# Gates, keys and queries of steps 10 to 23 turned by VectorE in 32x32 squares instead of by TensorE

## The chip, the core and the metric

The kernel runs on one core of a Trainium2 chip. The core's engines work side by side, each through its own queue of instructions in order: TensorE (PE, with its weight loads as PEld) multiplies matrices into the eight banks of PSUM, VectorE (DVE), ScalarE (ACT) and GpSimd (POOL) work on elements, SyncE (SP) issues the transfers from and to memory. [...] The metric is the device time of one execution in microseconds (us).

## The reference

Three stages follow each other, for 4 batches of 768 tokens (3072 in all), 8 heads of 48 features, model width 384:

```python
# attention with a gated state, per batch and head
f = 1 / (1 + exp(-f_logit))
for t in range(768):
    state = f[t, :, None] * state + outer(k[t], v[t])
    y[t] = q[t] @ state
x = y as (3072 tokens, 384)
# first network: 384 -> 2048 -> 384
h = x @ w_in;  x = (h * cos(h)) @ w_out
# second network: rms norm, 384 -> 1536 -> 384
xn = x / sqrt(mean(x * x) + 1e-6) * rms_g
g = xn @ w_gate
out = (g * sigmoid(g) * (xn @ w_val)) @ w_out2
```

## The kernel before

**Steps.** The attention runs in 24 steps of 128 tokens (6 to a batch), all 8 heads at once as four pairs, with the features of a pair on the 128 partitions (48 of each 64 used) and the tokens along the row. Gates, keys and queries lie in memory token by token, so each has to be turned. For that they are loaded as tiles `nat` with the tokens on the partitions, unused columns holding 16.0 (`load_nat`), two transfers to a tensor, and TensorE turns them with four 128x128 transposes each into a bank of PSUM (`turn1`, L198). From there a step does: `guard_f` (L214, ScalarE: sums up what is below the least gate allowed; at the end the sum decides between this program and a general one), `gates` (tanh, L219), `scan_end` (VectorE: the affine step from tanh to sigmoid L228, a scan from the last token backwards into `E` L229, two tiny instructions; GpSimd copies the scan's end, L234), `scan_start` (a scan of the gates, L238; GpSimd copies parts of v, L239), `scale_k` and `scale_q` (keys and queries times the scans, L246 and L253), the products on TensorE (`piece_pe`), the masked copy of the scores (`causal`, L390), the new state and its decayed copy, and the step's result split in two parts, `xh` and `xl`.

**Blocks and slots.** The first network works on blocks of 512 tokens (four steps), each in 16 slots, one for 128 hidden units. Steps 0 to 4 of the attention run ahead; steps 5 to 23 are spread over the slots of blocks 0 to 4, one of four pieces of a step to a slot. A slot's actions are written out in the string `SLOT[1]` (for blocks 1 to 4), and each engine gets its instructions in the order of that string:

- H: nine matmuls for the hidden units (L550), in one of two banks in turn; k, w, s, g: the rounding of the cosine's argument on ScalarE (L559), the rest on VectorE (L565), the cosine on ScalarE (L571), the product with H's bank on VectorE (L576), which then is free for the H two slots on
- hi and lo, a slot later: g in two parts, gh on ScalarE (L584) and gl on GpSimd (L591)
- P: the attention's piece on TensorE
- out: nine matmuls for the output, of the hidden units two slots back (L601), from gh and gl. They end a slot and aren't in the string
- kn, xh, xl, am, st, kt, qt, cy, tanh, grd, scan: what the attention does on the other engines after the piece of the slot before
- act, dv, pe, po: work put off to a slot of a given number, such as the evacuation of a finished block (`m1_evac`, L613, ScalarE, in slot 2 of the block after), its squares, and the column sum on TensorE (`m1_sum`, L628)

With n0 and p0 the step and piece of the slot before, the four slots of a step are called A to D here. **A** (p0 = 0): P is the scores (L301); kn; tanh, guard and `scan_end` of step n0+1. **B** (p0 = 1): P is the new state (L326; none in a batch's last step) and the turn of the next keys; the masked copies, `scan_start`. **C** (p0 = 2): P is the result (L344 to L362) and the turn of the next queries; `scale_k`, the state's addition. **D** (p0 = 3): P is the turn of the scaled keys (L291; none in a batch's last step) and the turn of the next gates; xh, xl, `scale_q`, the state's decay.

The attention's products and turns share three banks in rotation (`att_bank`; the column sum takes one, too). SP's queue holds all transfers in the order in which the program issues them: with each turn the load of the same tensor two steps on, the load of v, and the small transfers for the norm.

Of the kernel before, what the change touches and what calls it, by code (L numbers as in the profile page):

```python
# [9 lines left out]
F32 = mybir.dt.float32  # L10
# [3 lines left out]
AF = mybir.ActivationFunctionType  # L14
ALU = mybir.AluOpType
# [13 lines left out]

SLOT = (  # L30
    "tanh hi H t kn x kt xh xl qt cy am st scan P k f w x grd f s t lo g po",
    "tanh hi H kn kt xh xl qt cy am st scan P k w grd s lo act dv g pe po",
    "act H hi k w lo P dv t pe s x g f po",
)
SLOT2 = (
# [14 lines left out]
def kernel(  # L50
# [14 lines left out]
    nc = tc.nc  # L65
    B, H, S, D = q.shape
# [3 lines left out]
    C = 128  # L70
    NP = H // 2
    NCH = S // C
    NSTEP = B * NCH
# [3 lines left out]
    GT = 4  # L77
# [44 lines left out]
    att = ExitStack()  # L122
    ap_ = att.enter_context(tc.tile_pool(name="ap", bufs=1))
    HEAD = 4
    nats = [ap_.tile([128, KD, 512], F32, name=f"nat{x}") for x in range(2)]
    ft = [ap_.tile([128, NP * W + 1], F32, name="ft")]
    c1 = ap_.tile([128, NP * W + 1], F32, name="c1")
# [10 lines left out]
    def body(t):  # L138
        return t[:, 0:NP * W].rearrange("p (i t) -> p i t", i=NP)[:, :, 1:W]
# [39 lines left out]
    def load_nat(n, parts=range(3)):  # L179
# [4 lines left out]
        for x in parts:  # L184
            src = (f_logit, k, q)[x]
            for j in range(2):
                a = src[b, j::2, t0:t0 + C, :].rearrange("i t d -> t i d")
                nc.sync.dma_start(out=nat(n)[:, x, :, j, 0:D], in_=a)

    def turned(n, x):  # L190
        return bank[x] if n <= HEAD else st[n, "t", x]

    def turn1(n, x):

        if n > HEAD:
            st[n, "t", x] = att_bank()
        for i in range(NP):
            nc.tensor.transpose(  # L198
                turned(n, x)[:, C * i:C * (i + 1)],
                nat(n)[:, x, i].rearrange("p j e -> p (j e)"), ident,  # L200
            )

    def turn(n):
        for x in range(3):
# [4 lines left out]
    def heads(t):  # L209
        return t.rearrange("p (i t) -> p i t", i=NP)  # L210

    def guard_f(n):
        x = heads(turned(n, 0))
        nc.scalar.activation(  # L214
            out=x, in_=x, func=AF.Relu, scale=-1.0, bias=cb[:, 3:4], accum_out=low[:, n:n + 1]
        )

    def gates(n):
        nc.scalar.activation(  # L219
            out=body(ft[0]), in_=heads(turned(n, 0)), func=AF.Tanh, scale=0.5  # L220
        )

    def scan_end(n):

        f = ft[0]
        E = ap_.tile([128, NP * W], F32, tag="E", name="E")
        st[n, "E"] = E
        nc.vector.tensor_scalar(body(f), body(f), 0.5, 0.5, op0=ALU.mult, op1=ALU.add)  # L228
        nc.vector.tensor_tensor_scan(  # L229
            E[:, ::-1], f[:, NP * W:0:-1], c1[:, NP * W:0:-1], 0.0, op0=ALU.mult, op1=ALU.add  # L230
        )
        nc.vector.tensor_scalar(pads(d1), pads(E), P_LEAST, None, op0=ALU.max)
        nc.vector.reciprocal(out=pads(d1), in_=pads(d1))
        nc.gpsimd.tensor_copy(out=pall[:, n, :], in_=pads(E))  # L234

# [7 lines left out]

    def scale_k(n):
        kt = ap_.tile([128, NP, C], F32, tag="kt", name="kt", bufs=2)
        nc.vector.tensor_tensor(  # L246
            out=kt, in0=heads(turned(n, 1)), in1=body(st.pop((n, "E"))), op=ALU.mult
        )
        st[n, "kt"] = kt

    def scale_q(n):
        qt = ap_.tile([128, NP, C], F32, tag="qt", name="qt", bufs=2)
        nc.vector.tensor_tensor(  # L253
            out=qt, in0=heads(turned(n, 2)), in1=body(ft[0]), op=ALU.mult
        )
        nc.vector.memset(pads(ft[0]), 0.0)
        st[n, "qt"] = qt

# [27 lines left out]
    def piece_pe(n, p):  # L286
        if p == 0:
            if not last(n):
                t = st[n, "tr"] = att_bank()
                for i in range(NP):  # L290
                    nc.tensor.transpose(t[:, 128 * i:128 * (i + 1)], st[n, "kt"][:, i, :], ident)  # L291
            if n >= HEAD and n + 1 < NSTEP:
                turn1(n + 1, 0)
                load_nat(n + 3, (0,))
                load_v(n + 1)
        elif p == 1:
            t = [att_bank(), att_bank()]
            for i in range(NP):
                for j in range(2):
                    o = 64 * j  # L300
                    nc.tensor.matmul(  # L301
                        t[j][:, C * i:C * (i + 1)], st[n, "kt"][o:o + D, i, :],
                        st[n, "qt"][o:o + D, i, :], start=True, stop=True,
                    )
            st.pop((n, "kt"))
            st[n, "sc"] = t
        elif p == 2:
            zs(n)
            if n >= HEAD and n + 1 < NSTEP:
                turn1(n + 1, 1)  # L310
                load_nat(n + 3, (1,))
        else:
            ys(n)
            if n >= HEAD and n + 1 < NSTEP:
                turn1(n + 1, 2)
                load_nat(n + 3, (2,))

    def zs(n):
        if last(n):
# [461 lines left out]
    if True:  # L781
# [120 lines left out]
        for j, (t0, N) in enumerate(blocks):  # L902
# [21 lines left out]
            for i in range(N1):  # L924
# [7 lines left out]
                    "hi": lambda: gp and m1_hi(*gp),  # L932
                    "lo": lambda: gp and m1_lo(*gp),
                    "kn": lambda: p0 == 0 and not last(n0) and kn_evac(n0),
                    "tanh": lambda: p0 == 0 and more and gates(n0 + 1),
                    "grd": lambda: p0 == 0 and more and guard_f(n0 + 1),
                    "scan": lambda: more and (
                        p0 == 0 and scan_end(n0 + 1) or p0 == 1 and scan_start(n0 + 1)
                    ),
# [313 lines left out]
```

## Time and profile before

| | |
|---|---|
| median of 3 runs | 1054.02 us (1053.69 to 1055.05) |
| the profiled execution | 1053.78 us |
| its span, first to last instruction | 1052.0 us |
| TensorE busy | 1012.3 us (96%) |
| VectorE busy | 576.1 us (55%) |
| ScalarE busy | 421.3 us (40%) |
| GpSimd busy | 321.0 us (31%) |
| chain that ended last | TensorE 86%, VectorE 5%, ScalarE 2%, transfers 2% |

The busy time of TensorE is an average over stages, and since matmuls overlap, the length of a single one isn't what it adds to the queue. That is read from the distance between the starts of two neighbours.

### The profile page before, as it was taken

Reading aid. Unit: us, or ns where it says so; the run is one execution under the profiler, and the core shown is the slowest. Engines: PE = TensorE matmul, PEld = TensorE weight load, DVE = VectorE, ACT = ScalarE, POOL = GpSimd, SP = SyncE. Lnnn points to the kernel's source line nnn. Section 1 sums busy time; section 2 is a strip of 40 time slices with the busy share of each in tenths; the row PEclk is TensorE's granted clock in tenths of the full one; section 3 lists DMA queues with packets and bytes.
Section 4 is the critical chain, followed back from the end, with each engine's and each line's share of the span. In section 5 each row is a group of like instructions: output and inputs, shape, how many; then the busy total and the mean of one; then the engine's idle time right before and its main releaser. Section 6 shows DMA issues by size and latency. Waiting matters only on the chain.

```text
span 1052.0 us, 15791 instructions
## 1 busy us (share of the span) xinstructions
PE 1012.3 (96%) x6088; PEld 829.4 (79%) x6088; DVE 576.1 (55%) x904; ACT 421.3 (40%) x737; POOL 321.0 (31%) x366
## 2 busy tenths in 40 slices
PE   6778899999999999999999999999999999999997
PEld 5556677777777777777787788888888888888886
DVE  7888875555556655554377766435335335335222
ACT  2466655444444444444477554322222212212211
POOL 1555654432533433253377453201001001001000
PEclk9798999999999999999999999999999999999999
DMA  8865222121212212110234344332342343342000
GB/s 173 192 177 134 87 51 61 31 39 36 63 32 44 61 31 38 38 47 3 48 118 132 104 150 150 86 118 88 124 142 82 114 130 94 120 127 60 31 1 34
DMA packets 144016, 89.24 MB, mean 85 GB/s; under 512 B 110902, under 2 KB 123190, under 8 KB 143932
## 3 DMA queue, kind: packets, MB, share of 16 engines
q1 hardware_dynamic: 143932, 88.14, 31.7%
q8 instruction: 50, 0.82, 0.3%
q14 instruction: 34, 0.28, 0.1%
HBM read 78.66 MB, written 9.46 MB: 84 GB/s over the span
## 4 chain that ended last, share of the span: by engine, by line
PE 86%; DVE 5%; ACT 2%; DMA 2%; issue 2%; POOL 1%; SPq 1%; DVEq 0%; ACTq 0%; POOLq 0%
PE bank L703 29%; PE bank L601 17%; PE bank L550 16%; PE bank L739 14%; PE bank L198 2%; PE bank L301 1%; PE bank L350 1%; PE bank L344 1%; DMA nat<-in_k_dram 1%; DVE E L229 1%; PE bank L362 1%; PE bank L326 1%; PE bank L291 1%; POOL gl L591 1%; DMA v_sb<-in_v_dram 1%
## 5 line engine op out<-in xcount | busy, mean ns | idle before, releaser
L601 PE MATMUL bank<-gh,wo 128*128 128x512 f32 x576 | 206.8, 413 | 1.5 <-ACT x L613 1.2
L591 POOL TENSOR_TENSOR gl<-g,gh 128x512 fp32r<-128x512 f32 x96 | 126.7, 1320 | 167.0 <-ACT gh L584 163.8
L717 DVE SCALAR_TENSOR_TENSOR u<-bank,sg 128x512 f32<-128x512 f32 x72 | 49.7, 691 | 199.2 <-PE bank L703 199.2
L601 PEld LDWEIGHTS bank<-gh,wo 128*128 128x128 f32 x576 | 109.3, 190 | 28.1 <-ACT x L613 2.5
L703 PE MATMUL bank<-xh,wo 128*128 128x512 f32 x360 | 122.8, 395 | 0.0
L601 PE MATMUL bank<-gl,wo 128*128 128x512 f32 x288 | 115.8, 402 | 4.7 <-POOL gl L591 4.6
L712 ACT ACTIVATE sg<-bank 128x512 f32<-128x512 f32 x72 | 43.1, 599 | 171.8 <-PE bank L703 171.8
L687 POOL TENSOR_TENSOR xl<-x2b,xh 128x512 fp32r<-128x512 f32 x18 | 24.2, 1344 | 283.1 <-ACT xh L686 283.1
L724 ACT CAST uh<-u 128x512 fp32r<-128x512 f32 x72 | 44.7, 621 | 152.4 <-DVE u L717 152.2
L576 DVE SCALAR_TENSOR_TENSOR g<-bank,wrap 128x512 f32<-128x512 f32 x96 | 66.3, 691 | 69.4 <-ACT wrap L571 67.7
L565 DVE SCALAR_TENSOR_TENSOR wrap<-bank,kint 128x512 f32<-128x512 f32 x96 | 65.8, 685 | 69.8 <-ACT kint L559 69.7
L559 ACT ACTIVATE kint<-bank,cb 128x512 int32<-128x512 f32 x96 | 65.9, 687 | 83.4 <-PE bank L550 83.2
L571 ACT ACTIVATE wrap<-wrap,cb 128x512 f32<-128x512 f32 x96 | 69.5, 724 | 72.8 <-DVE wrap L565 70.9
L584 ACT CAST gh<-g 128x512 fp32r<-128x512 f32 x96 | 59.6, 621 | 92.2 <-PE bank L601 70.3
L703 PEld LDWEIGHTS bank<-xh,wo 128*128 128x128 f32 x360 | 67.6, 188 | 14.6
L730 DVE TENSOR_TENSOR ul<-u,uh 128x512 fp32r<-128x512 f32 x72 | 51.6, 716 | 48.9 <-ACT uh L724 48.9
L739 PE MATMUL bank<-wo,uh 128*128 128x384 f32 x288 | 74.1, 338 | 0.0
L703 PE MATMUL bank<-xl,wo 128*128 128x512 f32 x180 | 71.0, 394 | 0.0
L601 PEld LDWEIGHTS bank<-gl,wo 128*128 128x128 f32 x288 | 54.7, 190 | 18.8 <-POOL gl L591 7.8
L198 PE MATMUL bank<-ident,nat 128*128 128x128 f32 x288 | 45.8, 284 | 13.7 <-DVE xl L382 4.0
L739 PEld LDWEIGHTS bank<-wo,uh 128*128 128x128 f32 x288 | 52.6, 188 | 3.5 <-issue 0.5
L525 POOL TENSOR_TENSOR wo<-wx,wo 128x384 fp32r<-128x384 f32 x32 | 35.9, 1122 | 52.4 <-ACT wo L524 52.4
(334 smaller groups left out, 2190.8 us busy)
## 6 DMA issues: line engine op xcount, KB each, us to landing
stage<-in_moe_w_out_dram SPq DMA_DIRECT2D x56, 384.0 KB, 3.3
stage<-in_moe_w_gate_dram SPq DMA_DIRECT2D x24, 384.0 KB, 3.2
stage<-in_moe_w_val_dram SPq DMA_DIRECT2D x24, 384.0 KB, 3.7
stage<-in_moe_w_in_dram SPq DMA_DIRECT2D x16, 384.0 KB, 3.6
nat<-in_f_logit_dram SPq DMA_DIRECT2D x48, 96.0 KB, 3.8
nat<-in_k_dram SPq DMA_DIRECT2D x48, 96.0 KB, 2.8
nat<-in_q_dram SPq DMA_DIRECT2D x48, 96.0 KB, 2.2
v_sb<-in_v_dram SPq DMA_DIRECT2D x24, 192.0 KB, 3.7
```

Of the source, the lines that this page charges most:

```text
L198: nc.tensor.transpose(turned(n, x)[:, C * i:C * (i + 1)], nat(n)[:, x, i].rearrange("p j e -> p (j e)"), ident,)
L550: nc.tensor.matmul(t, l[:, 128 * kk:128 * (kk + 1)], r[:, kk, 0:N], start=idx == 0, stop=idx == 3 * KD - 1,)
L559: nc.scalar.activation(out=kt, in_=hb[j, i], func=AF.Identity, scale=INV2PI * UNIT, bias=cb[:, 0:1])
L565: nc.vector.scalar_tensor_tensor(out=w, in0=hb[j, i], scalar=INV2PI * UNIT, in1=kt, op0=ALU.mult, op1=ALU.subtract)
L571: nc.scalar.activation(out=w, in_=w, func=AF.Sin, scale=2.0 * math.pi, bias=cb[:, 1:2])
L576: nc.vector.scalar_tensor_tensor(out=g, in0=hb.pop((j, i)), scalar=UNIT, in1=w, op0=ALU.mult, op1=ALU.mult)
L584: nc.scalar.copy(out=h, in_=g)
L591: nc.gpsimd.tensor_tensor(out=l, in0=g, in1=h.bitcast(F32), op=ALU.subtract)
L601: nc.tensor.matmul(acc[m][:, 0:N], lw[:, cs], r, start=i == 0 and x == 0, stop=i == N1 - 1 and x == 2,)
L703: nc.tensor.matmul(t[y], l[:, 128 * kk:128 * (kk + 1)], r[:, kk, :], start=idx == 0, stop=idx == 3 * KD - 1,)
L730: nc.vector.tensor_tensor(out=l, in0=u, in1=h.bitcast(F32), op=ALU.subtract)
L739: nc.tensor.matmul(o2[tt][:, 0:DM], lu[:, cs], r, start=i == 0 and x == 0, stop=i == N2 - 1 and x == 2,)
```

## The change

From step 10 on (`FLIP`) the three tensors of a step are loaded so that one row of 192 elements holds four tokens of a head: partition p of the first 32 holds tokens 4p to 4p+3, and the next 32 partitions hold the same from feature 32 on (`load_raw`: four transfers to a tensor, into four buffers cut out of the old two). VectorE turns each tensor in squares of 32x32 (`flip`, one instruction for 128x512 elements), reading SBUF and writing the tile in which the tensor is then worked on: the gates' tile, the scaled keys, the scaled queries. The partitions beyond a head's 48 features then hold values of the next token, or the 16.0 of `clear_raw`. Steps up to 9 stay as they were. The guard writes its unused result to `E` in place of the bank. In blocks 1 to 4 the action `ff` (the gates' square turn) is new, tanh for these steps runs with the guard, behind k, and `scan` stands behind w. A load is issued as soon as the turn of its buffer's old content is in the queue.

```diff
 SLOT = (
     "tanh hi H t kn x kt xh xl qt cy am st scan P k f w x grd f s t lo g po",
-    "tanh hi H kn kt xh xl qt cy am st scan P k w grd s lo act dv g pe po",
+    "tanh hi H kn ff kt xh xl qt cy am st P k w grd scan s lo act dv g pe po",
     "act H hi k w lo P dv t pe s x g f po",
 )
 SLOT2 = (
...
     att = ExitStack()
     ap_ = att.enter_context(tc.tile_pool(name="ap", bufs=1))
     HEAD = 4
+    FLIP = 10
     nats = [ap_.tile([128, KD, 512], F32, name=f"nat{x}") for x in range(2)]
     ft = [ap_.tile([128, NP * W + 1], F32, name="ft")]
     c1 = ap_.tile([128, NP * W + 1], F32, name="c1")
...
                 a = src[b, j::2, t0:t0 + C, :].rearrange("i t d -> t i d")
                 nc.sync.dma_start(out=nat(n)[:, x, :, j, 0:D], in_=a)
+    raw = [
+        nats[x // 2].rearrange("p x t -> p (x t)")[:, NP * RUN * (x % 2):NP * RUN * (x % 2 + 1)]
+        .rearrange("p (i r) -> p i r", i=NP) for x in range(4)
+    ]
+    def clear_raw(x):
+        for o in (32, 96):
+            nc.gpsimd.memset(raw[x][o:o + 32, :, RUN - 32:RUN], 16.0)
+    def raw_of(n, x):
+        return raw[(3 * (n - FLIP) + x) % 4]
+    def load_raw(n, x):
+        if n >= NSTEP:
+            return
+        b, c = divmod(n, NCH)
+        t, src = raw_of(n, x), (f_logit, k, q)[x]
+        for j in range(2):
+            a = src[b, j::2, c * C:c * C + C, :].rearrange("i (p g) d -> p i (g d)", g=GT)
+            o = 64 * j
+            nc.sync.dma_start(out=t[o:o + 32], in_=a)
+            nc.sync.dma_start(out=t[o + 32:o + 64, :, 0:RUN - 32], in_=a[:, :, 32:RUN])
+    def flip(dst, n, x):
+        nc.vector.transpose(
+            out=dst.rearrange("p i (t g) -> p i g t", g=GT),
+            in_=raw_of(n, x).rearrange("p i (g d) -> p i g d", g=GT)[:, :, :, 0:32],
+        )
     def turned(n, x):
         return bank[x] if n <= HEAD else st[n, "t", x]
     def turn1(n, x):
+        if n >= FLIP:
+            return
         if n > HEAD:
             st[n, "t", x] = att_bank()
         for i in range(NP):
...
                 turned(n, x)[:, C * i:C * (i + 1)],
                 nat(n)[:, x, i].rearrange("p j e -> p (j e)"), ident,
             )
+        if HEAD < n < FLIP - 2:
+            load_nat(n + 2, (x,))
+        elif n == FLIP - 2 and x:
+            for y in ((), (0,), (1,))[x]:
+                clear_raw(y)
+                load_raw(FLIP, y)
+        elif n == FLIP - 1 and x:
+            for y in ((), (2,), (3,))[x]:
+                clear_raw(y)
+                load_raw(FLIP + y // 3, y % 3)
     def turn(n):
         for x in range(3):
...
     def heads(t):
         return t.rearrange("p (i t) -> p i t", i=NP)
+    def flip_f(n):
+        if n >= FLIP:
+            flip(body(ft[0]), n, 0)
+            load_raw(n + 1, 1)
     def guard_f(n):
+        if n >= FLIP:
+            E = st[n, "E"] = ap_.tile([128, NP * W], F32, tag="E", name="E")
+            nc.scalar.activation(
+                out=body(E), in_=body(ft[0]), func=AF.Relu, scale=-1.0, bias=cb[:, 3:4],
+                accum_out=low[:, n:n + 1],
+            )
+            return
         x = heads(turned(n, 0))
         nc.scalar.activation(
             out=x, in_=x, func=AF.Relu, scale=-1.0, bias=cb[:, 3:4], accum_out=low[:, n:n + 1]
         )
     def gates(n):
-        nc.scalar.activation(
-            out=body(ft[0]), in_=heads(turned(n, 0)), func=AF.Tanh, scale=0.5
-        )
+        x = body(ft[0]) if n >= FLIP else heads(turned(n, 0))
+        nc.scalar.activation(out=body(ft[0]), in_=x, func=AF.Tanh, scale=0.5)
     def scan_end(n):
         f = ft[0]
-        E = ap_.tile([128, NP * W], F32, tag="E", name="E")
-        st[n, "E"] = E
+        if n < FLIP:
+            st[n, "E"] = ap_.tile([128, NP * W], F32, tag="E", name="E")
+        E = st[n, "E"]
         nc.vector.tensor_scalar(body(f), body(f), 0.5, 0.5, op0=ALU.mult, op1=ALU.add)
         nc.vector.tensor_tensor_scan(
             E[:, ::-1], f[:, NP * W:0:-1], c1[:, NP * W:0:-1], 0.0, op0=ALU.mult, op1=ALU.add
...
     def scale_k(n):
         kt = ap_.tile([128, NP, C], F32, tag="kt", name="kt", bufs=2)
-        nc.vector.tensor_tensor(
-            out=kt, in0=heads(turned(n, 1)), in1=body(st.pop((n, "E"))), op=ALU.mult
-        )
+        x = heads(turned(n, 1)) if n < FLIP else kt
+        if n >= FLIP:
+            flip(kt, n, 1)
+            load_raw(n + 1, 2)
+        nc.vector.tensor_tensor(out=kt, in0=x, in1=body(st.pop((n, "E"))), op=ALU.mult)
         st[n, "kt"] = kt
     def scale_q(n):
         qt = ap_.tile([128, NP, C], F32, tag="qt", name="qt", bufs=2)
-        nc.vector.tensor_tensor(
-            out=qt, in0=heads(turned(n, 2)), in1=body(ft[0]), op=ALU.mult
-        )
+        x = heads(turned(n, 2)) if n < FLIP else qt
+        if n >= FLIP:
+            flip(qt, n, 2)
+            load_raw(n + 2, 0)
+        nc.vector.tensor_tensor(out=qt, in0=x, in1=body(ft[0]), op=ALU.mult)
         nc.vector.memset(pads(ft[0]), 0.0)
         st[n, "qt"] = qt
...
                     nc.tensor.transpose(t[:, 128 * i:128 * (i + 1)], st[n, "kt"][:, i, :], ident)
             if n >= HEAD and n + 1 < NSTEP:
                 turn1(n + 1, 0)
-                load_nat(n + 3, (0,))
                 load_v(n + 1)
         elif p == 1:
             t = [att_bank(), att_bank()]
...
             zs(n)
             if n >= HEAD and n + 1 < NSTEP:
                 turn1(n + 1, 1)
-                load_nat(n + 3, (1,))
         else:
             ys(n)
             if n >= HEAD and n + 1 < NSTEP:
                 turn1(n + 1, 2)
-                load_nat(n + 3, (2,))
     def zs(n):
         if last(n):
...
                     "hi": lambda: gp and m1_hi(*gp),
                     "lo": lambda: gp and m1_lo(*gp),
                     "kn": lambda: p0 == 0 and not last(n0) and kn_evac(n0),
-                    "tanh": lambda: p0 == 0 and more and gates(n0 + 1),
-                    "grd": lambda: p0 == 0 and more and guard_f(n0 + 1),
+                    "tanh": lambda: p0 == 0 and n0 + 1 < FLIP and gates(n0 + 1),
+                    "ff": lambda: p0 == 0 and more and flip_f(n0 + 1),
+                    "grd": lambda: p0 == 0 and more and (
+                        guard_f(n0 + 1), n0 + 1 >= FLIP and gates(n0 + 1)
+                    ),
                     "scan": lambda: more and (
                         p0 == 0 and scan_end(n0 + 1) or p0 == 1 and scan_start(n0 + 1)
                     ),
```

VectorE, from the affine step on the gates of slot A to the scaling of the keys in slot C; `ft` are the gates, `am` the masked scores, `wrap` and `g` the results of w and g. Before:

```order
L228 TENSOR_SCALAR ft<-ft 128x4x128
L229 SCALAR_TENSOR_TENSOR E<-ft,c_130 128x516
L232 TENSOR_SCALAR d_131<-E 128x4
L233 RECIPROCAL d_131<-d_131 128x4
L565 SCALAR_TENSOR_TENSOR wrap<-bank_77,kint 128x512
L576 SCALAR_TENSOR_TENSOR g<-bank_77,wrap 128x512
L390 COPY_PREDICATED am_132<-mask,bank_81 128x512
L390 COPY_PREDICATED am_133<-mask,bank_79 128x512
L238 SCALAR_TENSOR_TENSOR ft<-ft,d_131 128x516
L565 SCALAR_TENSOR_TENSOR wrap<-bank_78,kint 128x512
L576 SCALAR_TENSOR_TENSOR g<-bank_78,wrap 128x512
L246 TENSOR_TENSOR kt<-bank_81,E 128x512
```

The same stretch of VectorE's queue with the change (L216 is the square turn, L621 and L632 are w and g):

```order
L216 STREAM_TRANSPOSE ft<-nat_127 128x4x4x32
L621 SCALAR_TENSOR_TENSOR wrap<-bank_77,kint 128x512
L283 TENSOR_SCALAR ft<-ft 128x4x128
L284 SCALAR_TENSOR_TENSOR E<-ft,c_130 128x516
L287 TENSOR_SCALAR d_131<-E 128x4
L288 RECIPROCAL d_131<-d_131 128x4
L632 SCALAR_TENSOR_TENSOR g<-bank_77,wrap 128x512
L446 COPY_PREDICATED am_132<-mask,bank_80 128x512
L446 COPY_PREDICATED am_133<-mask,bank_81 128x512
L621 SCALAR_TENSOR_TENSOR wrap<-bank_78,kint 128x512
L293 SCALAR_TENSOR_TENSOR ft<-ft,d_131 128x516
L632 SCALAR_TENSOR_TENSOR g<-bank_78,wrap 128x512
```

The scan of `E` moved behind w, the scan of the gates (L238, now L293) behind w of slot B, and g of both slots now stands behind a scan. The keys' square turn and their scaling (L216, L305) come next in the queue, and the scaling reads `kt` where it read a bank.

ScalarE in slot A, before (`gh`, `kn`, k's `kint`, the guard L214, the cosine L571; the tanh L219 is the first):

```order
L219 ACTIVATE ft<-bank_80 128x4x128
L584 CAST gh<-g 128x512
L371 COPY kn<-bank_79 128x512
L559 ACTIVATE kint<-bank_77,cb 128x512
L214 ACTIVATE bank_80,low<-bank_80,cb 128x512
L571 ACTIVATE wrap<-wrap,cb 128x512
```

And with the change (L263 is the guard, L275 the tanh, L627 the cosine):

```order
L640 CAST gh<-g 128x512
L427 COPY kn<-bank_79 128x512
L615 ACTIVATE kint<-bank_77,cb 128x512
L263 ACTIVATE E,low<-ft,cb 128x4x128
L275 ACTIVATE ft<-ft 128x4x128
L627 ACTIVATE wrap<-wrap,cb 128x512
```

The tanh went from the head of the slot to behind the guard, and both now read SBUF.

TensorE in slot D, the last matmul of H, the turns, and the first of out; before:

```order
L550 MATMUL bank_78<-xl_122,wi3h 128x512
L291 MATMUL bank_79<-ident,kt 128x128 x4
L198 MATMUL bank_80<-ident,nat_127 128x128 x4
L601 MATMUL bank_74<-gh,wo 128x512
L601 MATMUL bank_74<-gl,wo 128x512
```

And with the change (L606 is H, L350 the turn of the scaled keys, L657 out):

```order
L606 MATMUL bank_78<-xl_122,wi3h 128x512
L350 MATMUL bank_79<-ident,kt 128x128 x4
L657 MATMUL bank_74<-gh,wo 128x512
L657 MATMUL bank_74<-gl,wo 128x512
L657 MATMUL bank_74<-gh,wo 128x512
```

The turn of the next gates is gone, and out follows the turn of the scaled keys at once.

## Rows read from the trace of the kernel before

**Rows 1.** Stretches: window, length, busy us of PE, PEld, DVE, ACT, POOL.

```profile
175.60:498.00 322.40, 319.31 (x2297) 249.22 (x2296) 180.92 (x293) 149.11 (x251) 125.20 (x160) 1.00 0.19 39
```

**Rows 2.** What TensorE waited for in the same stretch (us in total, times, longest).

```profile
PE bank L628 <- ACT bank L214: 1.7, 4, 0.4
PE bank L601 <- ACT x L613: 1.2, 1, 1.2
```

**Rows 3.** Groups by line, same stretch: the turns (count, busy us, mean ns).

```profile
L198 PE MATMUL bank<-ident,nat 128*128 128x128 f32 x168 | 26.7, 281 | 0.0
```

**Rows 4.** Timeline of TensorE, places in two steps (start us, us, instruction, count).

```profile
346.26 0.67 PE L326 MATMUL bank<-v_sb,kn 128*64 128x48 f32 x16
...
347.28 0.48 PE L601 MATMUL bank<-gh,wo 128*128 128x512 f32 x1
...
353.70 0.66 PE L198 MATMUL bank<-ident,nat 128*128 128x128 f32 x4
354.47 0.50 PE L601 MATMUL bank<-gh,wo 128*128 128x512 f32 x1
...
449.29 0.60 PE L198 MATMUL bank<-ident,nat 128*128 128x128 f32 x4
449.65 0.48 PE L601 MATMUL bank<-gh,wo 128*128 128x512 f32 x1
...
460.02 0.66 PE L198 MATMUL bank<-ident,nat 128*128 128x128 f32 x4
460.44 0.48 PE L601 MATMUL bank<-gh,wo 128*128 128x512 f32 x1
...
466.86 0.66 PE L198 MATMUL bank<-ident,nat 128*128 128x128 f32 x4
467.27 0.48 PE L601 MATMUL bank<-gh,wo 128*128 128x512 f32 x1
```

**Rows 5.** Timeline of VectorE, two steps (idle before and its releaser in brackets).

```profile
298.46 1.22 DVE L238 TENSOR_TENSOR_SCAN ft<-ft,d 128x516 f32<-128x516 f32 x1
...
338.84 0.42 DVE L228 TENSOR_SCALAR ft<-ft 128x512 f32<-128x512 f32 x1
...
340.77 0.18 DVE L233 RECIPROCAL d<-d 128x4 f32<-128x4 f32 x1
...
343.25 0.69 DVE L576 SCALAR_TENSOR_TENSOR g<-bank,wrap 128x512 f32<-128x512 f32 x1 [0.86 <-ACT wrap L571]
...
345.11 2.28 DVE L238 TENSOR_TENSOR_SCAN ft<-ft,d 128x516 f32<-128x516 f32 x1
...
349.43 0.68 DVE L246 TENSOR_TENSOR kt<-bank,E 128x512 f32<-128x512 f32 x1
350.03 0.34 DVE L406 TENSOR_TENSOR Sn<-Sn,bank 128x192 f32<-128x192 f32 x1
352.48 0.69 DVE L565 SCALAR_TENSOR_TENSOR wrap<-bank,kint 128x512 f32<-128x512 f32 x1 [2.11 <-ACT kint L559]
```

**Rows 6.** Costliest groups of the page: a VectorE pass over SBUF alone.

```profile
L730 DVE TENSOR_TENSOR ul<-u,uh 128x512 fp32r<-128x512 f32 x72 | 51.6, 716 | 48.9 <-ACT uh L724 48.9
```

**Rows 7.** Timeline of ScalarE in slot A of the same step.

```profile
338.03 0.58 ACT L219 ACTIVATE ft<-bank 128x512 f32<-128x512 f32 x1
...
340.98 0.69 ACT L559 ACTIVATE kint<-bank,cb 128x512 int32<-128x512 f32 x1 [0.86 <-PE bank L550]
341.56 0.65 ACT L214 ACTIVATE bank<-bank,cb 128x512 f32<-128x512 f32 x1
...
342.42 0.72 ACT L571 ACTIVATE wrap<-wrap,cb 128x512 f32<-128x512 f32 x1
```

**Rows 8.** Timeline of GpSimd in slots A and B of the same step.

```profile
340.74 1.27 POOL L591 TENSOR_TENSOR gl<-g,gh 128x512 fp32r<-128x512 f32 x1
...
345.00 1.29 POOL L591 TENSOR_TENSOR gl<-g,gh 128x512 fp32r<-128x512 f32 x1 [2.76 <-ACT gh L584]
```

**Rows 9.** Timeline of SP's queue in slot D: the loads of one tensor.

```profile
336.76 0.92 SPq L188 DMA_DIRECT2D nat<-in_f_logit_dram  x2
```

## What the change is predicted to do

> **What bounds the kernel now.** I first cut the span into stretches and read the one that the change touches, from the first turn of step 10 to just behind the last turn of step 23 [rows 1]. TensorE is busy 319.31 of its 322.40 us there, at a granted clock of 1.00, while VectorE is busy 180.92, ScalarE 149.11 and GpSimd 125.20. The list of what TensorE waited for in that stretch has two entries [rows 2]: four waits, 1.7 us in all, before the column sums of a block (L628, waiting for a guard on ScalarE, L214, to leave a bank) and one of 1.2 us for the evacuation of a block (L613). So TensorE sets the time here, and an instruction taken from it is worth its place in TensorE's queue, as long as nothing else becomes late. The steps are 22.6 us long (322.40 us hold 57 slots, 14.25 steps).
>
> I use the names of the slots A to D from the section on the kernel. H, out, P, k, w, s, g, gh, gl are the actions listed there.
>
> **What goes.** Steps 10 to 23 are 14 steps with three turns each, four transposes to a turn: 168 [rows 3], and 42 turns on TensorE. Their listed mean of 281 ns isn't their price, since they overlap; the price is the distance from a turn's start to the start of what follows [rows 4]: 449.29 to 449.65 is 0.36 us in slot D, 460.02 to 460.44 is 0.42 in B, 466.86 to 467.27 is 0.41 in C. A step thus loses 1.19 us of TensorE's queue, 14 steps 16.7 us. The order of the change's section shows that the turns are gone and that nothing takes their place on TensorE.
>
> The turned banks go too. Of the three banks in rotation, the one that L628 takes was a turned bank, held until the guard had read it, so its four waits should vanish: its bank is now the one of the turned keys (L291), which ScalarE copies out (kn) ahead of the same slot's k. That is 1.7 us.
>
> **What comes on VectorE.** 42 square turns of 128x512 elements. No row shows one. From below, the cheapest pass over 512 elements is the affine step on the gates, 0.42 us at 338.84 [rows 5]; from above, the longest row in these steps is a scan of 2.28 us at 345.11. The row nearest in kind is a single f32 pass over 512 elements in SBUF, 716 ns [rows 6]; I take 0.7 us and call it F. [...]
>
> VectorE's own budget: 180.92 us over 14.25 steps is 12.7 us a step. To this come waits that nothing of VectorE's can cover: w to g for the cosine, 0.86 us [rows 5], in slots C and D; xl for two passes of ScalarE (gh and xh) of the length seen in [rows 7], some 1.2; and in A now the wait for the tanh, some 0.7. With 0.6 us for the collisions named below that is about 16.9 + 3F us, 19.0 with F = 0.7, against a step of 22.6 - 1.2 = 21.4 on TensorE. VectorE stays under.
>
> **What moves: slot A.** Before, tanh ran ahead of k in ScalarE's queue and the scan ahead of w in VectorE's. Now guard and tanh stand behind k and the scan behind w. On the clock of the step at 338 us: k starts at 340.98, the guard at 341.56, and the place where the cosine started, 342.42, is now the tanh's [rows 7]; with its 0.58 us it ends at 343.0. The chain from L228 to the reciprocal took from 338.84 to 340.95; it now takes 343.1 to 345.2, and g, 0.69 us, ends at 345.9 and not 343.94: 1.9 us late. Who waits for that: gh of slot A, first in ScalarE's queue in B, ahead of B's k. H of B ends where z started, near 346.2, so gh (0.6 us) holds k for some 0.3 at most, and k has no reader on TensorE. The bank of A's g is wanted by H of slot C, which starts after the nine matmuls of the out that began at 347.28 [rows 4], some 2 us: free over 2 us early.
>
> GpSimd holds the closer case. The copy of the scan's end (L234) stands ahead of D's gl there, which began at 340.74, 1.9 us after L228 [rows 5, 8]; now gl runs from 345.0 to 346.3. It was done at 342.0. Its reader is the second matmul of out in slot B, which started at 347.28 [rows 4] and now 0.42 earlier, its second matmul 0.3 later, 347.15. About 0.9 us is left of over 5, so this costs nothing, but narrowly.
>
> **What moves: slots B to D.** In B: two masked copies (some 1.3 us), w, the scan of the gates, g. The scan took 1.22 us at 298.46 and 2.28 at 345.11, where gl had begun on GpSimd at 345.00 [rows 5, 8]: started behind a gl, it loses 1.06 us. From 345.9 that is g ready at 349.8 to 350.9; then the keys' turn (F), scaling (0.68), the state's addition (0.34), 351.5 to 352.6, against w of slot C, whose place is 352.48 - 0.42 = 352.06. Scaling of keys and queries used to read one operand from PSUM; now both lie in SBUF, as with the scan, so each of these 28 instructions lies between the old 0.68 and that plus the scan's loss of 1.06 us. In most steps the difference falls into VectorE's slack; where slot C is due it makes w up to 1.6 us late. [...]
>
> That matters in three steps. At the start of blocks 2, 3 and 4 the first out waits for the evacuation, which stands behind C's cosine: out starts at 354.47, 0.77 after the turn's start at 353.70 and not 0.41 [rows 4]. There the turn in C (0.41) is hidden, and I take it that w's delay eats B's 0.42 too: 3 x 0.83 = 2.5 us lost.
>
> **Transfers.** Each tensor of a step comes by four transfers, not two, so SP issues 12 and not 6 a step. Two took 0.92 us of SP's time [rows 9], so 12 take 5.5 us of a step's 21.4. A load now waits on SP for VectorE's turn of the same buffer, and v's load (behind the gates' load, in D) and the small transfers of the root mean square queue behind it. Each turn has its data loaded five or six slots, over 25 us, earlier; v is wanted two slots later. I cost this at nothing; without that cover every late load would stop VectorE in the middle of its queue.
>
> **The sum.** 16.7 + 1.7 - 2.5 = 15.9 us off the profiled execution's 1053.78 us (its span and 1.78 us around it): 1037.9. The median is 0.24 above that execution, so 1038.1 us. Everything behind block 4 keeps its order and shifts as a whole. With nothing lost in the three steps it is 1035.6; with 1.1 us more lost in each of them (w at its latest), and 0.2 in half of the 14 slots B, 1043.
>
> **The rivals.**
>
> *D's gl comes late* (slot B, out). For: the 0.9 us left. The chain is tanh, scan, L234, gl, and in the two steps without z even 0.6 us less is left [rows 4]. Against: all its members have rows, and GpSimd idles before it. If the chain is 1.4 us longer than I count, TensorE stands 0.5 us in each of 14 steps: 7 us, 1045.
>
> *VectorE takes the gain.* With F from 1.5 us, 16.9 + 3F passes 21.4 and TensorE waits for g and the banks of H; at 1.9 all of the saving is gone and the time is 1054. For: the turn's output goes out in steps of four elements and no row of its kind exists. Against: the pass with one source at 338.84 takes 0.42, and the row nearest in kind 0.72.
>
> *Slower.* The same place, past the deciding F = 1.9 us: at the scan's 2.28 a step is 16.9 + 6.8 = 23.7 us, 1.1 above the present one, in 14 steps 15 us: 1069.
>
> *The change isn't what it says*: the turned rows beyond the 48 features hold the next token's values, and before a constant. If they tripped the guard, the program's other branch would run as well and multiply the time. Those values are gates of the same input, so I give it no more than 1 in 100.
>
> **How the numbers follow.** The forecast holds with 0.73 (1034 to 1043), late gl with 0.11 (1043 to 1050), VectorE taking the gain with 0.07 (1046 to 1055), slower with 0.09 (the other branch in it). From 1034 to 1047 about 0.8 lies. A measurement of this kernel tells 0.2%, about 2 us, from no change: faster 0.87, same 0.04, slower 0.09.
>
> **What would show it.** The profile after should have 120 turns of L198's kind on TensorE and 42 on VectorE near 0.7 us; PE nearly solid in the same stretch, some 16 us shorter; no wait ahead of the column sums; waits for the evacuation longer at three places; g of slot A ending 1.9 us later against its H. It is wrong if TensorE waits for gl in slots B, if VectorE is solid, or if the turn takes over 1.5 us.

## The result and the profile after

The changed kernel takes 1039.89 us (median of 4 runs, 1038.93 to 1040.72), the one before on the same chip 1054.01; the ratio is 0.9864, with a 95% interval from 0.9847 to 0.9881. That is 14.1 us less, where 15.9 were forecast (1038.1; 1034 to 1043, and 1034 to 1047 with a chance of about 0.8).

The busy time of the engines over the whole span, from the page:

```profile
PE 996.0 (96%) x5920; PEld 812.7 (78%) x5920; DVE 622.0 (60%) x946; ACT 418.9 (40%) x737; POOL 324.4 (31%) x374
```

The stretch of [rows 1] in the kernel after (the same slots), and two short ones that are used below; the columns are as there, then the granted clock, the transfers' share and GB/s:

```profile
175.32:483.74 308.42, 303.94 (x2130) 233.16 (x2128) 227.77 (x335) 146.46 (x251) 125.95 (x161) 0.99 0.26 63
257.97:261.40 3.43, 3.43 (x10) 2.67 (x9) 0.00 (x0) 0.68 (x2) 0.00 (x0) 0.52 0.59 229
433.48:435.34 1.86, 1.86 (x9) 1.50 (x8) 0.00 (x0) 0.58 (x2) 0.00 (x0) 1.00 0.19 74
```

322.4 us have become 308.4, with 168 matmuls less on TensorE, which is still all but solid; VectorE does 46.9 us more. What TensorE waits for there, as in [rows 2]:

```profile
PE bank L657 <- ACT x L669: 4.3, 3, 2.0
PE bank L657 <- POOL gl L647: 0.2, 1, 0.2
```

The wait ahead of the column sums is gone, the one for the evacuation has grown from 1.2 to 4.3 us. TensorE in slots D and B, against the places of [rows 4]:

```profile
328.55 0.60 PE L350 MATMUL bank<-ident,kt 128*128 128x128 f32 x4
328.90 0.48 PE L657 MATMUL bank<-gh,wo 128*128 128x512 f32 x1
...
338.69 0.67 PE L382 MATMUL bank<-v_sb,kn 128*64 128x48 f32 x16
339.29 0.50 PE L657 MATMUL bank<-gh,wo 128*128 128x512 f32 x1
339.63 0.39 PE L657 MATMUL bank<-gl,wo 128*128 128x512 f32 x1
```

Out follows the turned keys after 0.35 us and the state after 0.60: no turn stands between, and nothing is waited for.

**A ruler.** Executions differ by up to three microseconds before the first changed slot: in the ten profiled ones shown here, slot 19 begins between 172.5 and 175.9 us. They differ by 1.6 us behind TensorE's last matmul, too; from slot 75 to that matmul all ten take 551.2 to 551.3 us. So I compare the stretch from the start of slot 19 to that of slot 75, which holds all changed slots: the distance between the first H matmul of the two, here in the kernel after. It comes from one execution of each kernel.

```profile
172.87 0.40 PE L606 MATMUL bank<-xh,wi3h 128*128 128x512 f32 x1
...
479.16 0.39 PE L606 MATMUL bank<-xh,wi11h 128*128 128x512 f32 x1
```

| kernel | slot 19 | slot 75 | stretch | slot 34 | slot 50 | slot 66 | median us |
|---|---|---|---|---|---|---|---|
| before | 173.15 | 493.44 | 320.29 | 7.21 | 7.22 | 7.22 | 1054.01 |
| after | 172.87 | 479.16 | 306.29 | 8.67 | 7.71 | 7.69 | 1039.89 |
| order only | 175.86 | 496.15 | 320.29 | 7.22 | 7.22 | 7.22 | 1054.66 |
| from step 17 | 174.73 | 487.19 | 312.46 | 7.22 | 7.25 | 7.68 | 1048.31 |
| copy for the turn | 173.83 | 480.81 | 306.98 | 8.78 | 7.25 | 7.24 | 1039.10 |
| turn done twice | 175.27 | 507.96 | 332.69 | 8.58 | 8.57 | 10.12 | 1069.65 |
| keys behind w | 172.54 | 479.84 | 307.30 | 8.79 | 7.23 | 7.24 | 1041.78 |
| after, evacuation ahead | 174.04 | 475.15 | 301.11 | 5.76 | 6.48 | 6.48 | 1035.56 |
| before, evacuation ahead | 173.15 | 491.00 | 317.85 | 5.74 | 6.83 | 6.83 | 1051.99 |
| after, evacuation and gl ahead | 172.91 | 472.88 | 299.97 | 5.76 | 6.48 | 6.48 | 1033.60 |

Slots 34, 50 and 66 are those of the evacuation (slot 34 belongs to a batch's first step, whose result takes 1.1 us less). The medians come from three sets of runs, each with the kernel before beside it: 1054.01 for the kernel after, 1054.60 for the four from the order alone to the turn done twice, 1054.18 for the last four.

### The profile page after: what moved, and what is told of

Its sections match the earlier page's. It is cut to its first block, busy times and chain, and to the rows that moved or that the text cites. A ratio compares the mean times of both kernels' runs of the same rounds, so it can differ in the third digit from the quotient of the medians.

```text
span 1037.2 us, 15616 instructions
## 1 busy us (share of the span) xinstructions
PE 996.0 (96%) x5920; PEld 812.7 (78%) x5920; DVE 622.0 (60%) x946; ACT 418.9 (40%) x737; POOL 324.4 (31%) x374
## 4 chain that ended last, share of the span: by engine, by line
PE 80%; DVE 9%; ACT 4%; issue 2%; DMA 2%; POOL 2%; SPq 1%; DVEq 0%; ACTq 0%; POOLq 0%
PE bank L759 29%; PE bank L657 16%; PE bank L795 15%; PE bank L606 13%; DVE E L284 1%; PE bank L359 1%; PE bank L406 1%; DVE wrap L621 1%; PE bank L400 1%; DVE g L632 1%; PE bank L418 1%; DVE wx L562 1%; DMA nat<-in_k_dram 1%; DVE ft L293 1%; ACT wrap L627 1%
## 5 line engine op out<-in xcount | busy, mean ns | idle before, releaser
L657 PE MATMUL bank<-gh,wo 128*128 128x512 f32 x576 | 207.4, 414 | 4.4 <-ACT x L669 4.3
L657 PEld LDWEIGHTS bank<-gh,wo 128*128 128x128 f32 x576 | 109.2, 190 | 34.0 <-ACT x L669 5.4
L657 PE MATMUL bank<-gl,wo 128*128 128x512 f32 x288 | 115.8, 402 | 6.5 <-POOL gl L647 6.4
L627 ACT ACTIVATE wrap<-wrap,cb 128x512 f32<-128x512 f32 x96 | 69.3, 722 | 88.1 <-DVE wrap L621 87.4
L632 DVE SCALAR_TENSOR_TENSOR g<-bank,wrap 128x512 f32<-128x512 f32 x96 | 65.6, 683 | 43.3 <-ACT wrap L627 41.5
L621 DVE SCALAR_TENSOR_TENSOR wrap<-bank,kint 128x512 f32<-128x512 f32 x96 | 65.8, 685 | 35.1 <-ACT kint L615 34.5
L657 PEld LDWEIGHTS bank<-gl,wo 128*128 128x128 f32 x288 | 54.7, 190 | 21.4 <-POOL gl L647 10.2
L490 DVE SCALAR_TENSOR_TENSOR wacc<-stage,wacc 128x384 int32<-128x384 int32 x68 | 50.8, 748 | 0.7
```

The lines of the kernel that those rows point to most:

```text
L490: nc.vector.scalar_tensor_tensor(out=wacc, in0=hi, scalar=1 << 30, in1=wacc, op0=ALU.bitwise_xor, op1=ALU.bitwise_and,)
L621: nc.vector.scalar_tensor_tensor(out=w, in0=hb[j, i], scalar=INV2PI * UNIT, in1=kt, op0=ALU.mult, op1=ALU.subtract)
L627: nc.scalar.activation(out=w, in_=w, func=AF.Sin, scale=2.0 * math.pi, bias=cb[:, 1:2])
L632: nc.vector.scalar_tensor_tensor(out=g, in0=hb.pop((j, i)), scalar=UNIT, in1=w, op0=ALU.mult, op1=ALU.mult)
L657: nc.tensor.matmul(acc[m][:, 0:N], lw[:, cs], r, start=i == 0 and x == 0, stop=i == N1 - 1 and x == 2,)
```

## The experiments

**The order alone.**

```diff
-    FLIP = 10
+    FLIP = 24
```

> The new order of blocks 1 to 4 (both scans behind w) with no square turn at all: every step is still turned by TensorE, loads as before. Theory (the gain is the turns' place in TensorE's queue, and the order only uses slack): within 1.5 us of the kernel before, 1053 to 1055.5, TensorE waiting at the same places. Rival (the order itself gives or takes several us, because the scans no longer stand ahead of w or because g comes late): over 3 us away from 1054.

1054.66 against 1054.60, ratio 0.9998 (0.9989 to 1.0007), and a stretch of 320.29 us, the same to the hundredth. TensorE waits as in [rows 2]:

```profile
PE bank L684 <- ACT bank L269: 1.7, 4, 0.4
PE bank L657 <- ACT x L669: 1.2, 1, 1.2
```

Moving both scans behind w is free. The theory holds, the rival falls. (The tanh stays in its old place here, so its move behind k isn't part of this run.)

**The change from step 17 on.**

```diff
-    FLIP = 10
+    FLIP = 17
```

(With an odd number the first loads of step 17 overwrite what step 16 had loaded, so step 16 is computed from wrong data.)

> The change from step 17 on instead of 10: 7 steps, 21 turns, two of the four column sums and one of the three late evacuations (the one in which TensorE's clock fell isn't among them). Theory (so much a step): 7 x 1.16 = 8.1, plus 2 x 0.49 for the sums, less 0.84 for one evacuation: 8.3 us off 1054.0, 1045.7; the other 7 steps are then worth only 5.8 of the 14.1, since the evacuation with the clock drop lies in them. Rival (a fixed gain or loss from the transition or from the order, the rest in proportion): 14.1 / 2 = 7.0 off, 1047.0, or further away.

The median is 6.3 us below the 1054.60 beside it (0.9943, 0.9929 to 0.9956), on the rival's side; the stretch is 7.83 us shorter, between theory (8.3) and rival (7.0). The profiled executions of the two kernels are 5.4 us apart, too; the 2.5 us that this lacks lie outside the stretch, 1.6 ahead of slot 19 and 1.0 behind TensorE's last matmul, which the change doesn't touch. So the slots have to decide. Those ahead of slot 47 are as long as before; from there on a plain slot D, B or C is shorter by the same 0.42, 0.39 and 0.35 us as in the changed kernel. The table shows what I had left out: slot 50 holds the turn of step 17's queries and is an evacuation's slot, 7.25 us where it was 7.22, so this turn's 0.35 is hidden. With it the account by slots gives 7.9. The gain is so much a turn, not a fixed sum.

**A copy in place of the turn.**

```diff
-        nc.vector.transpose(
+        nc.vector.tensor_copy(
```

> The square turn replaced by a VectorE copy through the same access patterns, which leaves the transposition itself out, so the output isn't the reference's. If the copy takes 0.3 to 0.7 us and not 1.10: Theory (VectorE's length shows only where C's w is late, in three evacuations, by 0.24 to 0.5 us each): 1 to 1.5 us faster than the changed kernel, up to 3 if the evacuation at 257 us no longer lets the clock fall: 1036.5 to 1039. Rival (the longer turn costs throughout): 3 x 14 x 0.5 = 20 us less, 1020.

0.9853 (0.9834 to 0.9871), not told apart from the changed kernel; the stretch is 0.7 us longer, not 1.0 to 1.5 shorter. The groups of VectorE in the stretch:

```profile
L216 DVE COPY qt<-nat 128x512 f32<-128x512 f32 x14 | 16.3, 1162 | 0.0
L305 DVE TENSOR_TENSOR kt<-kt,E 128x512 f32<-128x512 f32 x14 | 12.2, 870 | 0.5
...
L216 DVE COPY kt<-nat 128x512 f32<-128x512 f32 x14 | 11.6, 825 | 0.0
L216 DVE COPY ft<-nat 128x512 f32<-128x512 f32 x14 | 8.9, 636 | 0.0
```

Copies take 0.64 to 1.16 us in the mean, not the 0.3 to 0.7 I had counted on, and their length follows GpSimd: 24 of the 42 begin with no gl running there and take 0.61 to 0.67 us, the other 18 take what is left of a gl and some 0.5 us more. The square turn doesn't do that: in the kernel after, 18 of 42 begin with 0.48 to 1.15 us of a gl left, and they too take 1.08 to 1.15. A copy behind a gl in this run:

```profile
459.91 1.29 POOL L647 TENSOR_TENSOR gl<-g,gh 128x512 fp32r<-128x512 f32 x1
459.93 1.75 DVE L216 COPY qt<-nat 128x512 f32<-128x512 f32 x1
```

And a turn behind a gl, in the kernel after:

```profile
458.40 1.29 POOL L647 TENSOR_TENSOR gl<-g,gh 128x512 fp32r<-128x512 f32 x1
458.54 1.13 DVE L216 STREAM_TRANSPOSE qt<-nat 128x512 f32<-128x512 f32 x1
```

Slots 50 and 66 are 0.46 and 0.45 us shorter, and slots 34 and 35 together 0.2 (13.39 us against 13.60; the granted clock falls here too, to 0.56 in the mean of 3.9 us, but within slot 34 alone): 1.1 us, as the theory has it. But the column sums now wait for kn (1.1 us in two of them) and one out for gl (0.5), so that the stretch isn't shorter. The copies take 36.8 us in all and the turns 46.3, so by the rival some 9.5 us would have gone; the stretch shows none of it. A shorter pass on VectorE buys nothing here, so the turn's 1.10 us doesn't cost throughout.

**The turn twice.**

```diff
-        nc.vector.transpose(
+        for _ in range(2):
+            nc.vector.transpose(
...
```

> Every square turn is done twice, so F is 2.2 us and not 1.10; nothing else changes. By the prediction's budget (16.9 + 3F = 23.5 us a step against 21.4) the kernel gets slower than before: 14 x 2.1 = 29 us on top of 1039.9, 1069. By the slack in the changed kernel's trace (xl could start 2.0 us earlier in D, the guard 0.65 in A: 18.8 us a step on VectorE, 22.1 with the turns doubled): 14 x 0.7 = 10 us more, and up to 7 for three later evacuations: 1050 to 1057. If VectorE's slack hides it: 1040.

1069.65, ratio 1.0147 (1.0131 to 1.0162): slower than before, at the very number of the prediction's budget, and 13 us above the upper end of what I had read from the slack. But TensorE's waits show that the budget's number was met by luck:

```profile
PE bank L658 <- POOL gl L648: 10.1, 9, 2.0
PE bank L658 <- ACT x L670: 7.2, 3, 3.2
PE bank L685 <- ACT kn L428: 7.0, 4, 2.1
PE bank L383 <- DVE am L447: 1.2, 2, 0.6
```

A plain step (slots 44 to 47) takes 5.46 + 6.06 + 6.46 + 4.60 = 22.6 us: 1.1 above the changed kernel's and not 2.1. It is slot B that grows, where out waits for gl, which waits behind the scan: the way of the rival on D's gl. All slots B together add some 14 of the stretch's 26.4 us. The rest comes from the evacuations and, with 10 us, from the four sums, whose bank now hangs on kn. An estimated 4.7 us of all this is TensorE's clock: in slots 40, 66 and 72 the matmuls start 0.43 us apart for some 3.4 us, where 0.23 is usual, as they do in the kernel after while the granted clock is 0.50. Slot 66 takes 10.12 us and slot 50, with the same wait and no such fall, 8.57, and three times the difference is 4.7. VectorE is busy for 260.5 of the stretch's 332.7 us. So VectorE's lateness decides between a gain and a loss, and it reaches TensorE through GpSimd's and ScalarE's queues before VectorE is solid.

**The keys behind w.**

```diff
-    "tanh hi H kn ff kt xh xl qt cy am st P k w grd scan s lo act dv g pe po",
+    "tanh hi H kn ff xh xl qt cy am P k w grd scan kt st s lo act dv g pe po",
```

(In slot 18, the only slot C of blocks 1 to 4 in which TensorE still turns the next queries, the state is read after its bank has gone to that turn, so that state is wrong.)

> The changed kernel with the keys' square turn, their scaling and the state's addition moved behind w in blocks 1 to 4, so that w of slot C no longer stands behind them on VectorE. Theory (the three late evacuations come from that queue): w starts 0.24, 0.5 and 0.5 us earlier there, the stretch from slot 19 to slot 75 goes from 306.3 to 305.0 us, and to some 303.4 if TensorE's clock no longer falls after the first of them; 1037 to 1038.7. Rival (the evacuation is late for another reason, ScalarE's queue or the result's own length): unchanged, 1039.9.

1041.78 (0.9885, 0.9870 to 0.9900), a stretch 1.0 us longer than the changed kernel's, where the theory had it 1.3 to 2.9 shorter and the rival the same: neither number holds. Slots 50 and 66 are 0.48 and 0.45 us shorter, as expected from a w that is 0.5 earlier, and slots 34 and 35 together 0.2 (13.37 us against 13.60), though the clock falls there still, by the matmuls of slot 34's out, which start 0.43 us apart from 257.41 on; but elsewhere 2.2 us are added, above all where a sum waits for kn:

```profile
PE bank L657 <- ACT x L669: 3.2, 3, 1.8
PE bank L684 <- ACT kn L427: 1.1, 2, 0.7
```

So the late evacuations do come from VectorE's queue ahead of w, but the queue only moves. Now g is late, with it gh, and behind gh in ScalarE's queue kn, for whose bank the sum waits: in slot 40 kn starts 3.1 us behind the slot's first matmul and not 2.1 as in the changed kernel, right behind this gh:

```profile
289.39 0.62 ACT L640 CAST gh<-g 128x512 fp32r<-128x512 f32 x1 [0.88 <-DVE g L632]
289.92 0.58 ACT L427 COPY kn<-bank 128x512 f32<-128x512 f32 x1
```

As a remedy it fails.

**The evacuation ahead, after and before.**

```diff
-    "tanh hi H kn ff kt xh xl qt cy am st P k w grd scan s lo act dv g pe po",
+    "tanh hi H kn ff kt xh xl qt cy am st P k act w grd scan s lo dv g pe po",
```

> The changed kernel with a finished block's evacuation ahead of w and of the cosine, so that it waits for k alone; the cosine of four slots comes 1.6 us later. Theory: TensorE's three waits in the stretch go, and the clock drop with the first: slot 34 from 8.67 to 5.4 us (slot 58 has the same work without an evacuation and takes 5.38), slot 35 from 4.93 to 4.60, slots 50 and 66 from 7.7 to 6.48; the stretch falls from 306.3 to 300.2, slot 18 by 0.4 more: 1033.5. Rival (the wait moves to g or to the next out, since the cosine is late): under 3 us of it, 1037 or more.

> The same move of the evacuation in the kernel before, without the change. Theory: slot 34 from 7.21 to 5.74, slots 18, 50 and 66 by 0.39 each, 2.6 us together: 1051.4 where before takes 1054; with the evacuations out of the way the change is then worth 18, which is what the turns' places (16.2) and the sums' waits (1.9) give. Rival (the evacuation costs before as much as after, so it has no part in the shortfall): 6 us, 1048.

After: 1035.56 (0.9824, 0.9811 to 0.9838), its stretch 5.2 us shorter; slots 35, 50 and 66 go to 4.62, 6.48 and 6.48, as expected, slot 34 to 5.76, not quite to the 5.4 of a slot without an evacuation. Before: 1051.99 (0.9980, 0.9971 to 0.9989), its stretch 2.4 us shorter; slots 34, 50 and 66 at 5.74, 6.83 and 6.83. By the stretch both theories hold within a microsecond (by the median the first is 2 us off, 1035.56 against 1033.5), and both rivals fall. Between the two the change is worth 317.85 - 301.11 = 16.7 us instead of 14.0: the evacuation takes 2.7 us of it. The kernel with the change still waits, in its stretch:

```profile
PE bank L657 <- POOL gl L647: 0.7, 1, 0.7
PE bank L657 <- ACT x L669: 0.3, 1, 0.3
```

The 0.7 us are in slot 53, a step without the new state: out gets there 0.6 us early, and gl stands behind the scan's copy.

```profile
357.59 0.40 PE L657 MATMUL bank<-gh,wo 128*128 128x512 f32 x1
358.71 0.50 PE L657 MATMUL bank<-gl,wo 128*128 128x512 f32 x1 [0.72 <-POOL gl L647]
```

**The evacuation and gl ahead.**

```diff
-    "tanh hi H kn ff kt xh xl qt cy am st P k w grd scan s lo act dv g pe po",
+    "tanh hi lo H kn ff kt xh xl qt cy am st P k act w grd scan s dv g pe po",
```

> As the changed kernel with the evacuation ahead, and gl at the head of the slot too, so that on GpSimd it no longer stands behind the copy of the scan's end. Theory (gl in slot B waits only in the two steps without the new state, 0.2 to 0.4 us each): 0.4 us less than with the evacuation alone, 1033. Rival (gl ahead collides with VectorE's scans and scaled tensors, which then come late): 2 us or more slower than that.

1033.60 (0.9804, 0.9791 to 0.9818): the best, below both kernels. The stretch is 1.1 us shorter than with the evacuation alone, more than the 0.4 expected: slot 53 goes from 5.15 to 4.17 and slot 29 from 4.37 to 4.18. One wait is left:

```profile
PE bank L657 <- ACT x L669: 0.3, 1, 0.3
```

Against the kernel before with its evacuation ahead that is 317.85 - 299.97 = 17.9 us, about what the turns' places (14 x 1.16 = 16.2) and the sums' waits (1.9) give together. The kernel before with gl ahead as well wasn't run; with its evacuation ahead, its list of TensorE's waits in the stretch has no wait for gl, only the sums' 1.7 us.

## Why the prediction was right, and where it was off

**The turns' places: right, 16.7 forecast, 16.2 measured.** The slots of a plain step got shorter by 0.42 (D), 0.39 (B) and 0.35 us (C) where 0.36, 0.42 and 0.41 were read from the distances: 1.16 a step and not 1.19. The single prices were off by up to 0.06, D's too low, B's and C's too high, and that nearly cancels. The run with the order alone shows that moving the scans has no part in it, the slots of the one from step 17 on that it comes turn by turn. (The stretch of [rows 1] ends at 498.00, 7 us behind the last turn, which starts at 490.85, and not just behind it; the price of a turn doesn't hang on that.)

**The sums' waits: right.** 1.7 forecast, 4 x 0.49 measured, and the wait's row is gone.

**The turn's length: too short, within its bounds.** F is 1.10 us, not 0.7; scaled keys take 1.47 us in the mean, within the 0.68 to 1.74 given:

```profile
L305 DVE TENSOR_TENSOR kt<-kt,E 128x512 f32<-128x512 f32 x14 | 20.6, 1474 | 0.5
...
L216 DVE STREAM_TRANSPOSE qt<-nat 128x512 f32<-128x512 f32 x14 | 15.5, 1105 | 0.0
L216 DVE STREAM_TRANSPOSE ft<-nat 128x512 f32<-128x512 f32 x14 | 15.4, 1101 | 0.0
L216 DVE STREAM_TRANSPOSE kt<-nat 128x512 f32<-128x512 f32 x14 | 15.4, 1100 | 0.0
```

It cost nothing throughout: the budget (16.9 + 3.3 = 20.2 us) stays under the step's 21.5. The budget itself was too high, by about a microsecond at least: with the turn done twice it gives 23.5 us, and a plain step took 22.6.

**The path through slots A to C: right almost to the instruction.** ScalarE in slot A of the step that [rows 7] show:

```profile
333.66 0.69 ACT L615 ACTIVATE kint<-bank,cb 128x512 int32<-128x512 f32 x1
334.24 0.72 ACT L263 ACTIVATE E<-ft,cb 128x512 f32<-128x512 f32 x1
...
335.08 0.64 ACT L275 ACTIVATE ft<-ft 128x512 f32<-128x512 f32 x1
```

VectorE from there to w of slot C, against [rows 5]:

```profile
335.75 0.43 DVE L283 TENSOR_SCALAR ft<-ft 128x512 f32<-128x512 f32 x1 [0.68 <-ACT ft L275]
336.21 1.23 DVE L284 TENSOR_TENSOR_SCAN E<-ft,c 128x516 f32<-128x516 f32 x1
...
337.78 0.68 DVE L632 SCALAR_TENSOR_TENSOR g<-bank,wrap 128x512 f32<-128x512 f32 x1
...
340.40 1.25 DVE L293 TENSOR_TENSOR_SCAN ft<-ft,d 128x516 f32<-128x516 f32 x1
...
342.15 1.09 DVE L216 STREAM_TRANSPOSE kt<-nat 128x512 f32<-128x512 f32 x1
343.27 1.57 DVE L305 TENSOR_TENSOR kt<-kt,E 128x512 f32<-128x512 f32 x1
...
345.03 0.67 DVE L621 SCALAR_TENSOR_TENSOR wrap<-bank,kint 128x512 f32<-128x512 f32 x1
```

GpSimd's gl in the same slots, against [rows 8]:

```profile
337.67 1.29 POOL L647 TENSOR_TENSOR gl<-g,gh 128x512 fp32r<-128x512 f32 x1
...
339.25 1.31 POOL L647 TENSOR_TENSOR gl<-g,gh 128x512 fp32r<-128x512 f32 x1
343.01 1.28 POOL L647 TENSOR_TENSOR gl<-g,gh 128x512 fp32r<-128x512 f32 x1 [2.46 <-ACT gh L640]
```

From k's start to the end of A's g it is 4.8 us (4.9 forecast, 3.0 before). The scan of the gates takes 1.25 here and not 2.28: of the gl begun at 339.25 only 0.16 us are left when it starts, where 1.18 were left in [rows 5, 8]. The collision has moved to the scaled keys, 1.57 us behind the gl of 343.01, as the prediction's bound had it. (Ten of the 14 scaled keys begin with some 1.0 us of a gl left and take 1.55 to 1.59; the other four take 1.19 to 1.26.) D's gl ends at 338.96 and its matmul starts at 339.63, in the list of the result's section: 0.7 us to spare where 0.9 were counted, and in slot 53, without the new state, too late by 0.2. That narrow place was worth naming: once the evacuation was out of the way, it was the largest wait left.

**The transfers: right.** They were put at nothing, and in the stretch neither TensorE nor VectorE nor ScalarE has a wait for a transfer.

**The evacuations: the term that was mis-sized.** The prediction put "3 x 0.83 = 2.5 us lost", with the price of slot 50 for all three. Against the gains of the other slots, slots 50 and 66 lose 0.84 and 0.82, as forecast, but slots 34 and 35 lose 2.1, 3.8 in all. TensorE there:

```profile
257.40 0.50 PE L657 MATMUL bank<-gh,wo 128*128 128x512 f32 x1 [1.98 <-ACT x L669]
257.74 0.40 PE L657 MATMUL bank<-gl,wo 128*128 128x512 f32 x1
257.97 0.93 PE L657 MATMUL bank<-gh,wo 128*128 128x512 f32 x2
...
260.83 0.63 PE L606 MATMUL bank<-xh,wi3h 128*128 128x512 f32 x1
```

and in slot 66:

```profile
433.14 0.50 PE L657 MATMUL bank<-gh,wo 128*128 128x512 f32 x1 [1.14 <-ACT x L669]
...
435.34 0.39 PE L606 MATMUL bank<-xh,wi3h 128*128 128x512 f32 x1
```

From 257.97 on, half a microsecond after the wait of 1.98 us, the granted clock is 0.52 in the mean of 3.4 us, and 0.50 from 258.40 to 261.40; after the one of 1.14 it is 1.00. The nine matmuls of out take 257.40 to 260.83, 3.43 us, where slot 66 takes 2.20, and slot 35 takes 4.93 where 4.60 is usual: 1.23 + 0.33 = 1.56 us. Take these away and 2.2 us of lost evacuation are left, against 2.5. The rest of the shortfall is gl in slots B of the two steps without the new state, 0.15 and 0.40 us; with gl ahead both are gone.

In sum 16.2 + 1.9 - 3.8 - 0.5 = 13.8, by the ruler 14.0. So the forecast is 1.8 us off by the median, of which the clock, which the prediction doesn't have, is the largest part.

**The rivals.** D's gl came late in two slots of 14 only, 0.5 us of the 7 that it was priced at. VectorE takes no gain, as F stayed under 1.5. Slower is the way with a turn done twice, F = 2.2; that the time then meets the price is luck, since it came through gl, the sums, the evacuations and the clock. Had the turn taken twice its time, the forecast would have been wrong by 30 us, and no row ahead of the run ruled that out: the 0.7 was a pass of another kind.

**Still open.** Why the clock falls. In the copy and in the keys' run it fell at slot 34 too, after waits of 1.79 us each; with the turn done twice it fell after waits of 2.05 (slot 66) and 2.09 us (slots 40 and 72), but not after three of 2.04 us, nor at slot 34 after 3.16:

```profile
265.96 0.50 PE L658 MATMUL bank<-gh,wo 128*128 128x512 f32 x1 [3.16 <-ACT x L670]
```

So the length of the one wait ahead doesn't decide it. With the evacuation ahead there was no such fall in the stretch, in either kernel: with the change the granted clock is 1.00 from 177 to 480 us, and without it all matmuls of H follow each other after 0.22 to 0.24 us. Why the square turn takes 1.10 us is open as well; no run varied its shape.

## What to carry to other kernels

Price an instruction on a solid engine by the distance between its neighbours' starts, not by its listed duration (0.36 us for four transposes of 0.28 each), and check by slots what was won. Work moved to an engine with slack still made what stood behind it in that queue late here; look for the few slots in which something waits at the end of that queue, here an evacuation, for which TensorE's wait grew from 1.2 to 4.3 us and which could have gone first. Clear such places before measuring a change: the same change was worth 14.0 us with the evacuation in the way and 16.7 with it ahead in both kernels.

## What the runs showed of the hardware

A square turn of 128x512 f32 elements by VectorE took 1.08 to 1.15 us in all 42 cases, 1.5 times the f32 pass of [rows 6] (0.72), whether or not a gl ran on GpSimd. A copy through the same access patterns took 0.61 to 0.67 us with no gl running and 1.75 behind the gl of 459.91, so it wasn't the quicker stand-in I took it for. TensorE's granted clock was 0.52 over 3.4 us behind a wait of 2 us, and that cost 1.56 us, nearly as much as the wait itself.
